# MLP weights in runs of four, the bias loaded as rows, and products that stream 64 columns, at the end of a decode kernel

## The chip, the cores and the metric

The kernel runs on one core of one Trainium2 chip. The metric is device time in microseconds (us). A run also states its span, the time from the first to the last profiled instruction; the time is usually 1.3 to 1.6 us longer than the span. Because that difference has nothing to do with the instructions studied here, I quote spans beside times where tenths matter. All runs compared are fast; two runs near 672 us are slow and left out.

Words used: TensorE multiplies (the profile's PE is its products, PEld its weight loads), VectorE is DVE, ScalarE is ACT, SP issues most DMAs. "Landing" is the moment when the last of a DMA's shares has counted up its semaphore; the records show 16 such counts for each weight load. The "granted clock" is the share of TensorE's full clock that the record shows, here always 1.00 or 0.50.

## The reference

One decode step of a transformer layer for 4 sequences with one token each: attention over a cache of 4096 positions and 32 heads, then an MLP with the Mish activation.

```
x = A_x                                     # (4, 1, 640)
q = layernorm(x) @ wq                       # 640 -> 32 heads x 128
p = softmax(q . k_cache * 128**-0.5)        # 4 x 32 heads x 4096 positions
h = x + (p . v_cache) @ wo                  # 4096 -> 640
a = layernorm(h) @ w1 + b1                  # 640 -> 1728
a = a * tanh(softplus(a))
out = h + a @ w2                            # 1728 -> 640
```

In bf16 the two caches are 268 MB, the weights 15 MB. Everything must be read once.

## The kernel before

One DMA queue (SP) streams wq, then the K and V caches tile by tile, then wo, w1 and w2, in that order and nearly without a gap. The parts that matter here are the loads outside this queue and the work after the last V tile. In the wo and w1 products only 4 columns (the batch) are streamed against each 128 x 128 weight block:

```
FM = F // P                                   # 13 whole blocks of 128 MLP units, and 64 left over
# b1: unit 13*p + j sits at partition p, column j: 128 rows of 26 bytes, and 64 of 2 bytes
load(ac, b1T[:, 0:FM], B_b1[0 : FM * P].rearrange("(p j) -> p j", j=FM), "b1a", "S")
load(ac, b1T[0:FT, FM : FM + 1], B_b1[FM * P : F].rearrange("(p o) -> p o", o=1), "b1b", "S")
...
W2S = (0, 6, 10, 12, FM)                      # w2 arrives in chunks of 6, 4, 2 and 1 rows a partition
...
# attention output: 32 rows of wo, 5 blocks each
w = wo_sb[:, k, j, :].rearrange("p (m c) -> p c m", c=DC)[:, c, :]          # weight columns 5 apart: 10 bytes
mm(y_ps[:, c, :], w, a_t[:, k, j, :], False, done, "y" if done else None)   # 4 columns
...
# first MLP product: 14 blocks of units, 5 parts of the contraction, loaded as parts 0-1, 2-3, 4
w = w1_sb[:, c, 0 : FM * P].rearrange("p (f j) -> p j f", j=FM)[:, j, :]    # weight columns 13 apart: 26 bytes
mm(h1_ps[0 : (P if j < FM else FT), j, :], w, cen[:, c, :], False, done, ...)  # 4 columns
...
# second MLP product: the activations are the weights (4 columns), w2 streams 160 columns to each of 4 column strips
```

The softmax here doesn't subtract the row's maximum and nothing guards it: scores larger than these inputs give would overflow.

## Time and profile before

The median before was 662.52 us (662.31 to 663.42), the span of the profiled run 661.0 us.

The slice table of the page: the span in 40 slices, the granted TensorE clock and the busy share of the DMA engines in tenths, then the GB/s moved.

```profile
PEclk9998698879659796869668778977965879786865
DMA  9999999999999999999999999999999999999997
GB/s 386 444 440 444 421 408 445 437 441 437 429 420 440 436 436 436 440 428 424 444 432 432 440 428 424 444 432 433 444 436 432 424 440 428 440 440 428 412 418 303
```

DMA is at 9 (90% or more) in every slice but the last. This kernel lasts as long as its bytes take. The queue table says which queue: columns are packets, megabytes and the share of all 16 engines' time.

```profile
q1 hardware_dynamic: 6784, 283.27, 99.2%
q10 hardware_dynamic: 328, 0.09, 0.1%
```

Queue 1 is SP. Queue 10 belongs to ScalarE and carries x, the last 64 rows of w2, and b1. The DMA view lists issues with KB and the us from issue to landing; three lines of it:

```profile
slotA<-in_B_w_dram SPq DMA_DIRECT2D x1, 160.0 KB, 15.9
...
b1T<-in_B_b_dram ACTq DMA_DIRECT2D x1, 3.2 KB, 29.1
b1T<-in_B_b_dram ACTq DMA_DIRECT2D x1, 0.1 KB, 38.4
```

The last row of w2 (160 KB) is issued at 641.91 and lands at about 657.8; b1 lands 29 and 38 us after its issue at 3.4 and 3.8.

The chain of waits, cut to its last links (start, duration, what):

```profile
628.31 23.43 DMA slotB<-in_B_w_dram
...
651.78 3.07 PE red L714 x44
...
656.69 2.16 PE red L714 x55
...
658.87 0.33 DVE o_bf L710
```

Read backwards: o_bf, the output's conversion, waited for 2.16 us of TensorE (w2), that for the activation, and that for 3.07 us of TensorE (w1) which began when the second chunk of w1 had landed at 651.7. In this chain TensorE is the last thing that o_bf waits for. The timeline of TensorE shows the products themselves (start, duration, form, count, and in brackets the idle time before them):

```profile
638.95 1.76 PE L714 MATMUL y_ps<-a_t,slotB 128*128 128x4 bf16 x40
...
644.59 3.56 PE L714 MATMUL y_ps<-a_t,slotB 128*128 128x4 bf16 x80
...
649.76 3.93 PE L714 MATMUL red<-cen,slotB 128*64 128x4 bf16 x56 [0.30 <-DMA slotB<-in_B_w_dram]
...
653.74 1.10 PE L714 MATMUL red<-cen,slotB 128*64 128x4 bf16 x14
...
656.69 0.30 PE L714 MATMUL red<-w_tail,act 64*4 64x160 bf16 x4 [1.10 <-DVE act L703]
656.92 1.90 PE L714 MATMUL red<-slotA,act 128*4 128x160 bf16 x52
```

The 70 w1 products start 59 to 63 ns apart, the 160 wo products 40 ns apart, and four w2 products (one row) every 133 ns. o_bf began at 658.87, 1.03 us after the last row of w2 had landed (657.84 by the semaphore records).

The windows view, cut at the clock's own steps of 3.41 us (columns: window, its length, then busy time and instruction count of PE, PEld, DVE, ACT, POOL; granted clock; DMA share; GB/s):

```profile
639.85:643.26 3.41, 3.41 (x72) 3.38 (x70) 1.41 (x3) 1.10 (x1) 0.00 (x0) 1.00 1.01 426
643.26:646.67 3.41, 3.19 (x68) 2.89 (x66) 0.37 (x2) 0.00 (x0) 0.00 (x0) 0.50 1.01 413
646.67:650.09 3.42, 2.77 (x41) 2.51 (x40) 1.27 (x9) 0.18 (x1) 0.00 (x0) 0.50 1.01 417
650.09:653.50 3.41, 3.29 (x54) 3.19 (x53) 0.68 (x5) 1.40 (x2) 0.00 (x0) 0.50 1.04 432
653.50:656.90 3.40, 2.30 (x64) 1.89 (x62) 1.53 (x6) 0.25 (x1) 0.00 (x0) 0.50 0.84 334
```

The granted clock is 1.00 in one step and then 0.50 to the end, though PE is busy for 2.30 to 3.41 us of each step; most of the products stream 4 columns.

### The profile page before, as it was taken

The page shows a single profiled execution, that of the slowest core. Times are in us where ns is not written, and L with a number is a line of the kernel's source. Part 1 is how long each engine was busy: PE and PEld are TensorE (multiplying, and loading weights), DVE is VectorE, ACT ScalarE, POOL GpSimd, SP SyncE. Part 2 cuts the span into 40 slices and gives each one's busy share as a digit, 9 for nine tenths or more (in the row PEclk, how much of TensorE's full clock was granted, in tenths as well). Part 3 has the DMA queues.
Part 4 walks back from the last instruction along what each step waited for, and adds up shares of the span by engine and source line. Part 5 has one row for each costly group of instructions (what it writes and reads, how often), then busy time and mean ns, then how long its engine had stood idle before and what let it go on. Part 6 is the DMA issues. An engine that isn't in the chain of part 4 may idle for free. (4 is left out here: it accounts for less than half of the span.)

```text
span 661.0 us, 4948 instructions
## 1 busy us (share of the span) xinstructions
PE 386.6 (58%) x2623; PEld 70.5 (11%) x1663; DVE 407.4 (62%) x255; ACT 40.7 (6%) x157; POOL 1.7 (0%) x12
## 2 busy tenths in 40 slices
PE   0356667457317595838307485828534757675877
PEld 0100010101101010101100010100110001010146
DVE  2067889386049778677219688948306798857612
ACT  0200000000000000000000000000000000000011
POOL 0000000000000000000000000000000000000000
PEclk9998698879659796869668778977965879786865
DMA  9999999999999999999999999999999999999997
GB/s 386 444 440 444 421 408 445 437 441 437 429 420 440 436 436 436 440 428 424 444 432 432 440 428 424 444 432 433 444 436 432 424 440 428 440 440 428 412 418 303
DMA packets 7121, 283.48 MB, mean 429 GB/s; under 512 B 1028, under 2 KB 1352, under 8 KB 2376
## 3 DMA queue, kind: packets, MB, share of 16 engines
q1 hardware_dynamic: 6784, 283.27, 99.2%
q10 hardware_dynamic: 328, 0.09, 0.1%
q8 instruction: 6, 0.10, 0.1%
q14 instruction: 3, 0.02, 0.0%
HBM read 283.35 MB, written 0.01 MB: 429 GB/s over the span
## 5 line engine op out<-in xcount | busy, mean ns | idle before, releaser
L513 DVE TENSOR_TENSOR slotA<-slotA,q_bc 128x8192 bf16<-128x8192 bf16 x32 | 140.6, 4415 | 106.2 <-DMA slotA<-in_A_k_cache_dram 106.2
L513 DVE TENSOR_TENSOR slotB<-slotB,q_bc 128x8192 bf16<-128x8192 bf16 x32 | 140.7, 4416 | 17.6 <-DMA slotB<-in_A_k_cache_dram 17.6
L524 DVE TENSOR_REDUCE s_f<-red 128x64 f32<-128x1024 f32 x64 | 78.0, 1218 | 96.8 <-PE red L724 96.8
L724 PE MATMUL red<-slotA,ident 128*128 128x512 bf16 x480 | 135.3, 445 | 0.0
L724 PE MATMUL red<-slotB,ident 128*128 128x512 bf16 x480 | 127.4, 425 | 0.0
L714 PE MATMUL red<-slotA,ident 128*128 128x512 bf16 x32 | 14.4, 451 | 127.7 <-PEq L49 127.7
L714 PE MATMUL pv<-slotC,e 128*32 128x512 bf16 x768 | 52.9, 436 | 37.4 <-PEq L49 34.4
L714 PE MATMUL red<-slotB,ident 128*128 128x512 bf16 x32 | 14.1, 441 | 88.3 <-PEq L49 88.3
L393 ACT ACTIVATE ex<-s_f 128x64 bf16<-128x64 f32 x64 | 16.4, 256 | 513.3 <-DVE s_f L524 513.3
L538 DVE TENSOR_TENSOR e<-ex,hmask 128x512 bf16<-128x512 bf16 x64 | 39.8, 683 | 0.0
L714 PEld LDWEIGHTS pv<-slotC,e 128*32 128x32 bf16 x768 | 22.6, 107 | 94.3 <-issue 80.7
L714 PEld LDWEIGHTS red<-slotA,ident 128*128 128x128 bf16 x32 | 3.2, 99 | 195.7 <-issue 195.7
L714 PEld LDWEIGHTS red<-slotB,ident 128*128 128x128 bf16 x32 | 3.2, 99 | 172.1 <-issue 172.1
L714 PEld LDWEIGHTS o_ps<-pv_sb,selo 128*32 128x32 f32 x136 | 13.5, 109 | 64.5 <-issue 64.5
L714 PE MATMUL o_ps<-pv_sb,selo 128*32 128x128 f32 x136 | 18.0, 276 | 0.0
L714 PE MATMUL pv<-slotA,e 128*32 128x512 bf16 x256 | 14.5, 380 | 0.3 <-PEq L49 0.3
L403 ACT COPY pv_sb<-pv 128x512 f32<-128x512 f32 x16 | 9.4, 585 | 68.6 <-PE pv L714 68.6
L393 ACT ACTIVATION_READ_ACCUMULATOR ex<-s_f 128x1 f32 x64 | 11.9, 186 | 0.0
L714 PEld LDWEIGHTS pv<-slotA,e 128*32 128x32 bf16 x256 | 6.7, 97 | 23.4 <-issue 17.5
L563 DVE RECIPROCAL rl<-misc 32x1 f32<-32x1 f32 x4 | 0.6, 150 | 12.7 <-PE misc L714 12.7
L714 PE MATMUL red<-slotC,lnT 128*32 128x512 bf16 x40 | 4.5, 629 | 6.7 <-PEq L49 6.7
L714 PE MATMUL y_ps<-a_t,slotB 128*128 128x4 bf16 x160 | 7.0, 179 | 0.2
(99 smaller groups left out, 67.2 us busy)
## 6 DMA issues: line engine op xcount, KB each, us to landing
slotC<-in_A_v_cache_dram SPq DMA_DIRECT2D x2, 4096.0 KB, 39.3
slotC<-in_A_wq_dram SPq DMA_DIRECT2D x1, 5120.0 KB, 16.4
slotB<-in_A_wo_dram SPq DMA_DIRECT2D x3, 1280.0 KB, 15.9
slotB<-in_B_w_dram SPq DMA_DIRECT2D x2, 864.0 KB, 22.6
slotA<-in_B_w_dram SPq DMA_DIRECT2D x1, 960.0 KB, 20.8
slotB<-in_A_wo_dram SPq DMA_DIRECT2D x1, 640.0 KB, 19.6
slotA<-in_B_w_dram SPq DMA_DIRECT2D x1, 640.0 KB, 19.7
slotB<-in_A_wo_dram SPq DMA_DIRECT2D x1, 480.0 KB, 20.3
```

What stands on the lines that cost most here:

```text
L393: lambda: a.activation(out=ex[:, sl], in_=s_f[:, sl], func=ACT.Exp, scale=SCALE, accum_out=rs[:, b, s : s + 1],),
L403: lambda: a.copy(out=pv_sb[:, :, :].rearrange("p r d -> p (r d)"), in_=pv[:, :]),
L513: lambda: v.tensor_tensor(out=t, in0=t, in1=q_bc[:, hg, b, :].unsqueeze(1).to_broadcast([P, RS, Dh]), op=ALU.mult,),
L524: lambda: v.tensor_reduce(out=s_f[:, s * RS : (s + 1) * RS], in_=red[:, k : k + 2, :].rearrange("p k (r c) -> p (k r) c", c=CW), axis=AX.X ...
L538: lambda: v.tensor_tensor(out=e[:, sl, :], in0=ex[:, sl].unsqueeze(2).to_broadcast([P, RS, G]), in1=hmask[:, :].unsqueeze(1).to_broadcast( ...
L563: dv.do(lambda: v.reciprocal(out=rl[:, :], in_=l_ps), ("rl", hg), DV)
L714: lambda: nc.tensor.matmul(out_, lhsT=lhsT, rhs=rhs, start=start, stop=stop, skip_group_check=skip),
L724: return t.add_instruction(mybir.InstMatmult(name=nc.get_next_instruction_name(), engine=mybir.EngineType.PE, ins=[t.lower_ap(rhs), t.lowe ...
```

## The change

The intent: w1 products that start less than 60 ns apart, by weight columns 8 bytes apart instead of 26; a TensorE clock that stays at 1.00 beyond 643.26, by wider products; and no 192 tiny DMA packets, by b1 as rows. The w2 rows follow the new order of units, in chunks of 4, 4, 4 and 1 rows.

```diff
+    FI = 4                    # units in runs of 4
+    FB = FM // FI
+    F0 = FB * FI * P
+    WD = 16                   # batch columns repeated 16 times
+    y_w = y_full[:, 0 : DC * WD * N].rearrange("p (c w n) -> p c w n", w=WD, n=N)
+    y_ps = y_w[:, :, 0, :]
+    h1_w = red[:, 2:4, :].rearrange("p k (j w n) -> p (k j) w n", w=WD, n=N)
+    h1_ps = h1_w[:, 0:FC, 0, :]
-    W2S = (0, 6, 10, 12, FM)
+    W2S = tuple(range(0, FM, FI)) + (FM,)
...
-            sp.need(("PV", i - 1) if hg else ("qb", N - 1))
+            sp.need(("PV", i - 1) if hg else "b1p")
...
-        load(ac, b1T[:, 0:FM], B_b1[0 : FM * P].rearrange("(p j) -> p j", j=FM), "b1a", "S")
-        load(ac, b1T[0:FT, FM : FM + 1], B_b1[FM * P : F].rearrange("(p o) -> p o", o=1), "b1b", "S")
+        load(ac, b1r[:, :], B_b1[0:F0].rearrange("(k f) -> k f", k=FB), "b1a", "B0")
+        load(ac, b1e[:, :], B_b1[F0:F].rearrange("(o f) -> o f", o=1), "b1b", "B1")
...                            # six small transposes on TensorE and two copies make b1T
-                    mm(y_ps[:, c, :], w, a_t[:, k, j, :], False, done, "y" if done else None)
+                    mm(
+                        y_w[:, c, :, :], w, a_t[:, k, j, :].unsqueeze(1).to_broadcast([P, WD, N]),
+                        False, done, "y" if done else None,
+                    )
-        mm(red[:, 2, 0 : FC * N], ident[:, :], zeros[:, 0 : FC * N], True, False)
+        for k in (2, 3):
+            mm(red[:, k, :], ident[:, :], zeros[:, 0:1].to_broadcast([P, 512]), True, False)
...
-                        w = w1_sb[:, c, 0 : FM * P].rearrange("p (f j) -> p j f", j=FM)[:, j, :]
+                        k, i = divmod(j, FI)
+                        w = w1_sb[:, c, k * FI * P : (k + 1) * FI * P]
+                        w = w.rearrange("p (f i) -> p i f", i=FI)[:, i, :]
...
-                        h1_ps[0 : (P if j < FM else FT), j, :], w, cen[:, c, :], False, done,
+                        h1_w[0 : (P if j < FM else FT), j, :, :], w,
+                        cen[:, c, :].unsqueeze(1).to_broadcast([P, WD, N]), False, done,
...                            # cut: loads of w2, start of y, bias products, semaphores
```

More of the change, by code (lines that the diff above doesn't have):

```diff
@@ L122 @@
     WSEM = ["WQ", "WT"] + [f"W{k}" for k in range(13)]
-    for s in ["PE", "DV", "DVP", "DVA", "AC", "ACP", "PO", "KA", "KB", "VA", "VC", "V2", "X", "S", "OUT0", "OUT1", "FIN"] + WSEM:
+    for s in ["PE", "DV", "DVP", "DVA", "AC", "ACP", "PO", "KA", "KB", "VA", "VC", "V2", "X", "B0", "B1", "OUT0", "OUT1", "FIN"] + WSEM:
         book.handles[s] = nc.alloc_semaphore(s)
@@ L173 @@
     wq = slot["C"][:, 0 : DC * H * Dh].rearrange("p (c n) -> p c n", c=DC)
+    b1r = sb("b1r", (FB, FI * P), BF16, setup, topC)
+    b1e = sb("b1e", (1, F - F0), BF16, setup, topC)
     x_bf = sb("x_bf", (N, D), BF16, setup, topC)
@@ L222 @@
     y_full = nc.alloc_psum_tensor("y_ps", (P, 512), FP32).ap()
-    y_ps = y_full[:, 0 : DC * N].rearrange("p (c n) -> p c n", n=N)
+    WD = 16
+    y_w = y_full[:, 0 : DC * WD * N].rearrange("p (c w n) -> p c w n", w=WD, n=N)
+    y_ps = y_w[:, :, 0, :]
     tpl = misc[:, 0 : DC * N].rearrange("p (c n) -> p c n", n=N)
@@ L226 @@
     l_ps = misc[0:BG, 64:65]
+    b1_ps = pv[:, 0:FC]
     a_ps = misc[:, 128 : 128 + G * N].rearrange("p (j n) -> p j n", n=N)
@@ L229 @@
     sq_ps = pv[:, 0 : DC * N]
-    h1_ps = red[:, 2, 0 : FC * N].rearrange("p (j n) -> p j n", n=N)
+    h1_w = red[:, 2:4, :].rearrange("p k (j w n) -> p (k j) w n", w=WD, n=N)
+    h1_ps = h1_w[:, 0:FC, 0, :]
     y2_ps = red[:, 0, 0:OC]
@@ L246 @@
     dv = Prog(nc.vector, book)
-    pe = Prog(nc.tensor, book, take=["DVP", "DVA", "ACP", "VA", "VC", "V2"] + WSEM)
+    pe = Prog(nc.tensor, book, take=["DVP", "DVA", "ACP", "VA", "VC", "V2"] + WSEM + ["B0", "B1"])
     def tiles(src, i):
@@ L330, in sync_prog @@
         sp.need(("PV", NT - 2))
-        w2_v = B_w2[0 : FM * P, :].rearrange("(p j) n -> p j n", j=FM)
         for k, (j0, j1) in enumerate(zip(W2S, W2S[1:])):
-            load(sp, w2_sb[:, j0:j1, :], w2_v[:, j0:j1, :], ("w2", j0), f"W{len(WOS) + len(W1S) - 1 + k}")
+            load(
+                sp, w2_sb[:, j0:j1, :],
+                B_w2[j0 * P : j1 * P, :].rearrange("(p j) n -> p j n", j=j1 - j0), ("w2", j0),
+                f"W{len(WOS) + len(W1S) - 1 + k}",
+            )
         store(sp, 0)
@@ L357, in act_prog @@
         a = nc.scalar
-        ac.need("b1z")
-        load(ac, b1T[:, 0:FM], B_b1[0 : FM * P].rearrange("(p j) -> p j", j=FM), "b1a", "S")
-        load(ac, b1T[0:FT, FM : FM + 1], B_b1[FM * P : F].rearrange("(p o) -> p o", o=1), "b1b", "S")
+        load(ac, b1r[:, :], B_b1[0:F0].rearrange("(k f) -> k f", k=FB), "b1a", "B0")
+        load(ac, b1e[:, :], B_b1[F0:F].rearrange("(o f) -> o f", o=1), "b1b", "B1")
         ac.need("eps", "mv")
@@ L504, in dve_prog @@
         dv.do(lambda: v.tensor_copy(out=xT[:, :, :], in_=tpx[:, :, :]), "xT", DVP)
+        dv.need("b1p", "b1z")
+        dv.do(lambda: v.tensor_copy(out=b1T[:, 0:FM], in_=b1_ps[:, 0:FM]), "b1m", DV)
+        dv.do(lambda: v.tensor_copy(out=b1T[0:FT, FM:FC], in_=b1_ps[0:FT, FM:FC]), "b1T", DVP)
         dv.do(lambda: v.memset(rsm[:, :, :], 1.0), ("rsm", -1), DVP)
@@ L649, in dve_prog @@
         dv.do(lambda: v.tensor_copy(out=h_hi[:, :, :], in_=st[:, :, :]), "h_hi", DV)
-        dv.need("std2", "b1b")
+        dv.need("std2")
         dv.do(
@@ L749, in pe_setup @@
         pe.need("xT")
-        mm(y_full[:, 0 : DC * N], ident[:, :], xT[:, :, :].rearrange("p c n -> p (c n)"), True, False)
+        mm(y_w, ident[:, :], xT[:, :, :].unsqueeze(2).to_broadcast([P, DC, WD, N]), True, False)
         pe.need("lnT", "wq")
@@ L768, in pe_setup @@
             )
+        pe.need("b1a", "b1b")
+        for k in range(FI):
+            mm(
+                b1_ps[:, k : FB * FI : FI], b1r[:, :].rearrange("k (f i) -> k i f", i=FI)[:, k, :],
+                ident[0:FB, 0:FB], True, True,
+            )
+        mm(b1_ps[:, FM - 1 : FM], b1e[:, 0:P], ident[0:1, 0:1], True, True)
+        mm(b1_ps[0:FT, FM:FC], b1e[:, P : P + FT], ident[0:1, 0:1], True, True, "b1p")
     def fold(i, s):
@@ L856, in wo_mm @@
                     done = k == NHG - 1 and j == G - 1 and c == DC - 1
-                    mm(y_ps[:, c, :], w, a_t[:, k, j, :], False, done, "y" if done else None)
+                    mm(
+                        y_w[:, c, :, :], w, a_t[:, k, j, :].unsqueeze(1).to_broadcast([P, WD, N]),
+                        False, done, "y" if done else None,
+                    )
         hg = NHG - 1
@@ L879, in pe_tail @@
                 for part in (b1_hi, b1_lo):
-                    mm(
-                        red[:, 2, 0 : FC * N], ident[:, :], part[:, :, :].rearrange("p j n -> p (j n)"),
-                        False, False,
-                    )
+                    for j0, j1 in ((0, FC // 2 + 1), (FC // 2 + 1, FC)):
+                        mm(h1_ps[:, j0:j1, :], ident[:, :], part[:, j0:j1, :], False, False)
             pe.need(("w1", c0))
@@ L886, in pe_tail @@
                 for c in range(c0, c1):
-                    if j < FM:
-                        w = w1_sb[:, c, 0 : FM * P].rearrange("p (f j) -> p j f", j=FM)[:, j, :]
+                    if j < FB * FI:
+                        k, i = divmod(j, FI)
+                        w = w1_sb[:, c, k * FI * P : (k + 1) * FI * P]
+                        w = w.rearrange("p (f i) -> p i f", i=FI)[:, i, :]
                     else:
-                        w = w1_sb[:, c, FM * P : F]
+                        w = w1_sb[:, c, j * P : min((j + 1) * P, F)]
                     done = c == DC - 1 and j == FM - 1
                     mm(
-                        h1_ps[0 : (P if j < FM else FT), j, :], w, cen[:, c, :], False, done,
+                        h1_w[0 : (P if j < FM else FT), j, :, :], w,
+                        cen[:, c, :].unsqueeze(1).to_broadcast([P, WD, N]), False, done,
                         "h1_ps" if done else None,
@@ L926, in pe_prog @@
         pe_setup()
-        pe.need("selo", "xT")
+        pe.need("selo", "xT", "b1T")
         logs = []
```

## The prediction

> **What bounds the kernel now.** The DMA stream. The slice table shows DMA at 9 tenths or more in all slices but the last, mean 429 GB/s, 283.48 MB, 99.2% on one queue. By the trace's landing records the last weight chunk (one row of w2) lands at 657.84 us of a 661.0 us span. The change moves none of these bytes and touches none of the waits that pace the K/V loads.
>
> **The tail.** The chain of waits ends: DMA of w1 until 651.7, TensorE 3.07, VectorE/ScalarE activation 1.8, TensorE w2 2.16 (to 658.85), o_bf 0.33, store. With w2's last row landing at 657.84, even a free TensorE could start o_bf only near 658.2, not 658.87. That 0.65 us, 0.1% of the span, is the most that the tail can give.
>
> **The change.**
> - w1 weights at a column step of 8 bytes instead of 26. In the timeline w1 products start every 59 to 63 ns; wo products (step 10 bytes) every 40 ns at either clock; the om transposes (step 16 bytes) every 62. [...]
> - 64 streamed columns instead of 4. The windows view grants 1.00 from 639.85 to 643.26, then 0.50 to the end. [...] the trace shows only these two, in steps of 3.41 us. Counting streamed columns in this trace, a step at full clock keeps it above about 0.35. The repeated wo (estimate 0.4 to 0.55) should keep it; layernorm gap and w1 (estimate 0.28) are a toss-up. At half clock a product takes about 53 ns (512 columns take 427), so wo 2 and 3 would lose up to 1 us; at full clock nothing. If it holds to w2, a w2 row goes from 133 ns to about 70.
> - Zeroing two full banks: about +0.5 us TensorE. Two more bias products: 0.1 us.
> - b1 as 4 rows: the 192 packets took 1.73 us summed over 16 engines, 0.1 us of stream; they landed at 42 us, needed at 650. Small transposes and the V(0) load now wait for b1; I expect it by 22 us, before qb at 23.6, while K(1) is in flight to 55: free.
> - w2 chunks of 4,4,4,1 rows for 6,4,2,1: same bytes; rows 8 to 11 arrive near 657.45.
>
> **On the critical path.** w1's second chunk lands at 651.73, its third at 652.80, so w1 can end near 653.6 to 654.1 instead of 654.76. w2 then starts near 655.7 and waits for landings. Of some 3 us of TensorE work saved, 0.3 to 0.65 us reach the end; if the clock falls during wo, about nothing.
>
> **Prediction.** 662.0 us (before 662.52), 8 in 10 between 661.3 and 662.9. Faster by over 2%: 0.01; within 2%: 0.98; slower: 0.01.
>
> **What would show it.** w1 products every 33 to 40 ns at full clock (53 at half); clock 1.0 from 643 to 647; last w2 landing still 657.5 to 658.1; a chain that ends with the DMA of w2 just before the last products, o_bf near 658.2 to 658.5; DMA share unchanged.
>
> **What would make it wrong.** b1 landing after 35 us, holding the first products; the last landing moving by a microsecond (16 KB instruction fetches take 0.95 us each; two fell after 646); the clock at half, so that wo runs late.

The forecast came to 662.0 us: of some 3 us of TensorE work saved, 0.3 to 0.65 us were to reach the end. By the paces that the runs below measured, 33 ns instead of 60, the 70 w1 products are worth up to 1.9 us; the 13 w2 rows, at 69 ns instead of 133, make another 0.8. The 33 in "What would show it" was my estimate.

## The result and the profile after

The median after was 661.38 us (661.26 to 662.32, 4 runs) against 662.41 us before. The ratio is 0.9984 with a 95% interval of 0.9967 to 1.0001; a ratio here is the mean time of one kernel's fast runs over that of the other's of the same rounds, so not quite the ratio of the medians quoted. The verdict is "same" at the 2% level. The medians lie 1.0 us apart, which is twice the predicted 0.5 us. The interval includes no difference at all. The spans show one more clearly: nine runs of the kernel after (here and in its repetition below) have 659.8 to 660.8, median 660.0, and 34 of the kernel before 660.6 to 661.3, median 661.0.

The queue table after:

```profile
q1 hardware_dynamic: 6784, 283.27, 99.4%
...
q10 hardware_dynamic: 112, 0.09, 0.0%
```

Queue 10 went from 328 packets to 112; SP's queue is unchanged. The chain of waits now ends with the stream:

```profile
639.18 17.80 DMA slotA<-in_B_w_dram
...
657.02 0.68 PE red L728 x20
...
657.73 0.32 DVE o_bf L724
```

The third chunk of w2 lands at 656.98, then TensorE needs only 0.68 us, and o_bf follows at 657.73. TensorE in the tail:

```profile
638.32 1.78 PE L728 MATMUL y_ps<-a_t,slotB 128*128 128x64 bf16 x40
...
644.12 3.61 PE L728 MATMUL y_ps<-a_t,slotB 128*128 128x64 bf16 x80
...
649.35 1.19 PE L728 MATMUL red<-cen,slotB 128*64 128x64 bf16 x28 [0.65 <-DMA slotB<-in_B_w_dram]
651.32 1.64 PE L728 MATMUL red<-cen,slotB 128*64 128x64 bf16 x28 [0.78 <-DMA slotB<-in_B_w_dram]
...
652.99 1.08 PE L728 MATMUL red<-cen,slotB 128*64 128x64 bf16 x14
...
655.92 0.24 PE L728 MATMUL red<-w_tail,act 64*4 64x160 bf16 x4 [1.09 <-DVE act L717]
656.09 0.72 PE L728 MATMUL red<-slotA,act 128*4 128x160 bf16 x32
657.02 0.65 PE L728 MATMUL red<-slotA,act 128*4 128x160 bf16 x20 [0.21 <-DMA slotA<-in_B_w_dram]
```

The wo products kept their 40 ns and are no slower for 16 times the columns. The first w1 chunk starts a product every 33 ns, most of the second and all of the third every 53 ns. A w2 row takes 69 ns instead of 133, and TensorE now idles 0.21 us for the landing of the third chunk. The windows at this run's clock steps:

```profile
641.50:644.90 3.40, 3.20 (x64) 2.83 (x63) 1.49 (x3) 0.00 (x0) 0.00 (x0) 1.00 0.98 409
644.90:648.30 3.40, 3.06 (x67) 2.84 (x65) 0.44 (x3) 0.00 (x0) 0.00 (x0) 1.00 1.04 425
648.30:651.70 3.40, 1.97 (x39) 1.69 (x39) 1.43 (x11) 1.58 (x2) 0.00 (x0) 1.00 1.00 416
651.70:655.10 3.40, 3.13 (x84) 2.76 (x81) 0.82 (x4) 0.25 (x1) 0.00 (x0) 0.51 1.02 416
655.10:658.50 3.40, 1.54 (x56) 0.93 (x56) 1.04 (x3) 0.00 (x0) 0.00 (x0) 0.99 0.32 127
```

The clock was 1.00 until 651.75, fell to 0.50 for one step, and was back at 1.00 for w2. The two w1 paces go with it: the products start 33 ns apart up to 651.75 and 53 ns apart after it. For 64 columns at half clock, 53 ns is also what I estimate from the cache phase, where 512 columns take 427 ns at that clock (216 at full). The 33 ns is also the pace of e3 below, with 4 columns at half clock.

From the semaphore records I took the landings and o_bf of both profiles. "Mean" is the mean over the 16 shares of the last DMA, which scatters less than the slowest share.

```
                          before    after
last w2 row, mean share   656.85    656.55     -0.30
last w2 row, landing      657.84    657.39     -0.45
o_bf starts               658.87    657.73     -1.14
landing to o_bf             1.03      0.34     -0.69
span                      661.02    659.86     -1.16
```

Two things came together: the stream ended earlier, and TensorE followed it more closely. How much of the first belongs to the change is settled under e2.

### The profile page after: what moved, and what is told of

The parts are those of the page before. It is cut to its first block, busy times and chain, and to the rows that moved or that the text cites. A ratio compares the mean times of both kernels' runs of the same rounds, so it can differ in the third digit from the quotient of the medians.

```text
span 659.9 us, 4968 instructions
## 1 busy us (share of the span) xinstructions
PE 382.4 (58%) x2630; PEld 68.6 (10%) x1672; DVE 407.7 (62%) x257; ACT 40.7 (6%) x157; POOL 1.7 (0%) x12
## 5 line engine op out<-in xcount | busy, mean ns | idle before, releaser
L738 PE MATMUL red<-slotA,ident 128*128 128x512 bf16 x480 | 137.3, 450 | 0.0
L738 PE MATMUL red<-slotB,ident 128*128 128x512 bf16 x480 | 124.5, 418 | 0.0
L728 PE MATMUL red<-slotA,ident 128*128 128x512 bf16 x32 | 14.5, 452 | 128.5 <-PEq L49 128.5
L728 PE MATMUL red<-slotB,ident 128*128 128x512 bf16 x32 | 14.0, 437 | 86.9 <-PEq L49 86.9
L517 DVE CAST b1T<-pv 128x13 bf16<-128x13 f32 x1 | 0.2, 174 | 13.1 <-PE pv L728 13.1
```

The source lines that it names most:

```text
L517: dv.do(lambda: v.tensor_copy(out=b1T[:, 0:FM], in_=b1_ps[:, 0:FM]), "b1m", DV)
L728: lambda: nc.tensor.matmul(out_, lhsT=lhsT, rhs=rhs, start=start, stop=stop, skip_group_check=skip),
L738: return t.add_instruction(mybir.InstMatmult(name=nc.get_next_instruction_name(), engine=mybir.EngineType.PE, ins=[t.lower_ap(rhs), t.lowe ...
```

## The experiments

My theory: the end is the last landing plus what TensorE still has to do. The b1 packets move the landing; runs of 4, the columns and the clock move the rest. The rivals are that the earlier landing is scatter between executions, that one part alone does everything, and that TensorE still limits the tail after the change. All times are medians of fast runs. Each group of runs was timed against the kernel before on the same chip, at 662.46, 662.53 and 662.52 us; 34 fast runs of it in these groups have spans of 660.6 to 661.3, median 661.0.

### e1: only b1 as a row

```diff
 # on the kernel before
-        load(ac, b1T[:, 0:FM], ...)          # 128 rows of 26 bytes
-        load(ac, b1T[0:FT, FM : FM + 1], ...) # 64 rows of 2 bytes
+        load(ac, b1r[:, :], B_b1.rearrange("(o f) -> o f", o=1), "b1a", "B0")
+        # 14 small transposes on TensorE after qb, two copies into b1T
```

> The kernel before with b1 loaded as one row and transposed on TensorE; weights and columns as before. The step from before to after was 1.0 us, of which the profiles put 0.69 us after the last w2 landing and 0.45 us into an earlier last landing (657.84 to 657.39). Theory A (the 192 tiny b1 packets cost the stream 0.45 us): the last w2 landing comes near 657.4 and the time falls by 0.45 us to about 662.0. Theory B (they cost only their own 1.73 us over 16 engines, 0.1 us, and the rest is scatter of the first loads): the landing follows the landing of wq, K(0) minus wq is about 0.1 us shorter, time lower by 0.1 us only. Distance from landing to o_bf stays 1.0 us in both.

Measured: 662.07 us (the reported median of 662.17 includes the slow run), spans 660.6 to 661.1, median 660.7. In the profile the mean share of the last landing is 656.58 and o_bf starts 1.02 us after the landing. So the stream ends earlier and the work after it has not moved. In time it is 0.3 to 0.4 us, between the 0.45 us of theory A and the 0.1 us of theory B. The test that was named for theory B came out for it: from the mean share of wq's landing to that of K(0)'s it is 19.29 us here and 19.39 in the kernel before, 0.10 us shorter. The landing of wq itself came 0.21 us earlier than in the profile before (15.19 against 15.40).

### e2: four copies of the tiny loads added

```diff
 # on the kernel after
+        for k in range(4):
+            load(ac, b1d[:, k, 0:FM], B_b1[0 : FM * P].rearrange("(p j) -> p j", j=FM), ("b1x", k), "S")
+            load(ac, b1d[0:FT, k, FM : FM + 1], B_b1[FM * P : F].rearrange("(p o) -> p o", o=1), ("b1y", k), "S")
...
-        dv.need("std2")
+        dv.need("std2", ("b1y", 3))
```

> The kernel after with four copies of the old b1 loads (768 tiny packets) added into a tile nobody reads, waited for late. Theory A: 0.45 us for each 192 packets, so the last landing and the time move by +1.8 us (about 663.2). Theory B: 0.1 us each, +0.4 us (about 661.8). If packets are free: 661.4.

Measured: 662.45 us, span median 660.9, which is 1.07 us and 0.9 us over the kernel after: between the theories again. The mean shares of the landings say more, if the last one is measured from that of wq:

```
copies  run             wq      last w2 row   between
0       after           15.18   656.55        641.37
0       after again     15.19   656.55        641.36
0       e1              15.19   656.58        641.39
0       e3              15.32   656.68        641.36
0       e5              15.07   656.34        641.27
0       e7              15.15   656.50        641.35
1       before          15.40   656.85        641.45
1       before again    15.27   656.71        641.44
1       e4              15.19   656.88        641.69
4       e2              15.17   657.45        642.28
```

Without copies the mean between the two is 641.35 us. One copy adds 0.10 and 0.09 us in the two profiles of the kernel before and 0.34 in e4; four add 0.93, or 0.23 each. The packets themselves are booked at 9 ns each, 1.73 us for 192, or 0.11 us when spread over 16 engines. So theory B's 0.1 us is what the kernel before paid; e2 and e4 paid more, 0.23 and 0.34 for each copy. The rest of the difference in last landings was there when wq landed. Most of it is older than the packets: the 80 KB of w2 that precede them in their queue landed (mean share) at 12.83 and 12.70 us in the kernel before and at 12.48 to 12.76 in the other eight, and the first tiny packet moved at 13.13. Of the landing's 0.45 us in the first pair of profiles, 0.21 is this earlier wq, 0.08 lies between wq and the last row, and 0.15 is scatter of the slowest share. Only the 0.08 can be put down to the packets.

The packet records of the kernel before show why b1 took so long to land: its 128 packets of 26 bytes stretch from 13.1 to 29.6 us, and from 14.6 us on they come back every 2.42 us, which is the length of one 64 KB packet of the SP queue. Whether each such change of queue costs time beyond the packet, and why e4 paid more than the kernel before for the same packets, stays open; no run here measures it by itself.

### e3: the kernel after with 4 columns

```diff
 # on the kernel after
-    WD = 16
+    WD = 1
-    h1_w = red[:, 2:4, :].rearrange("p k (j w n) -> p (k j) w n", w=WD, n=N)
+    h1_w = red[:, 2, 0 : FC * N].rearrange("p (j w n) -> p j w n", w=WD, n=N)
-        for k in (2, 3):
-            mm(red[:, k, :], ident[:, :], zeros[:, 0:1].to_broadcast([P, 512]), True, False)
+        mm(red[:, 2, 0 : FC * N], ident[:, :], zeros[:, 0 : FC * N], True, False)
...            # the bias products in one piece again
```

> The kernel after with 4 streamed columns again, runs of 4 and b1 rows kept. Theory that both parts are needed: granted clock 0.5 from about 643 on; wo 40 ns, w1 about 33 ns, a w2 row 133 ns; w1 ends earlier than in after (653.2 against 654.0, as 53 ns products vanish), but the last four w2 rows at 133 ns and the slower end put o_bf about 0.6 us after the last landing instead of 0.34: time +0.2 to +0.3 us on after. Rival (the columns gave most of the 0.69 us): landing to o_bf back near 1.0 us, +0.6 us.

Measured: 661.63 us, spans 660.1 to 660.4, median 660.1. TensorE:

```profile
649.62 1.16 PE L728 MATMUL red<-cen,slotB 128*64 128x4 bf16 x28 [0.29 <-DMA slotB<-in_B_w_dram]
...
652.83 0.73 PE L728 MATMUL red<-cen,slotB 128*64 128x4 bf16 x14
...
655.65 1.24 PE L728 MATMUL red<-slotA,act 128*4 128x160 bf16 x32
657.30 0.84 PE L728 MATMUL red<-slotA,act 128*4 128x160 bf16 x20 [0.41 <-DMA slotA<-in_B_w_dram]
```

The clock was 0.50 from 641.6 on. The w1 products still start 33 ns apart within a chunk: the same pace at half clock as the first chunk had at full clock in the kernel after. The w2 rows take 133 ns, and o_bf starts 0.53 us after the landing, so my theory of this run holds. The span is only 0.1 us over the median of the kernel after. The step from e1 (span 660.7, step of 26 bytes, 4 columns, one row of b1) to e3 (660.1) is the runs of 4 with their chunks of w2: 0.6 us, the largest single part of the change. No run separates the step from the chunks. The traces speak for the step: w2's first product (the 64-row tail) starts at 655.42 here and at 656.31 in e1, because w1 ends earlier.

### e4: only the 64 columns

```diff
 # on the kernel before
+    WD = 16                                   # y_w, h1_w, wide zeroing as in the change
-                    mm(y_ps[:, c, :], w, a_t[:, k, j, :], ...)
+                    mm(y_w[:, c, :, :], w, a_t[:, k, j, :].unsqueeze(1).to_broadcast([P, WD, N]), ...)
-                        h1_ps[0 : (P if j < FM else FT), j, :], w, cen[:, c, :], ...
+                        h1_w[0 : (P if j < FM else FT), j, :, :], w, cen[:, c, :].unsqueeze(1).to_broadcast([P, WD, N]), ...
```

> The kernel before with 64 streamed columns alone; w1 step 26 bytes and tiny b1 loads stay. If the last landing is a floor that either part almost reaches: w1 near 60 ns, clock 1.0 at w2 or not by chance, o_bf 0.35 to 0.65 us after the last landing, time 0.4 to 0.6 us below before. If the runs of 4 are what matters: landing to o_bf stays near 1.0 us and the time is that of before.

Measured: 662.54 us, span median 661.0: the kernel before. The expected 0.4 to 0.6 us did not come; the runs of 4 are what matters.

```profile
649.96 4.02 PE L717 MATMUL red<-cen,slotB 128*64 128x64 bf16 x56 [0.44 <-DMA slotB<-in_B_w_dram]
...
657.29 1.90 PE L717 MATMUL red<-slotA,act 128*4 128x160 bf16 x52
```

The w1 products stay at 60 ns, so w1 ends later than its last chunk lands, and w2 cannot start before 657.05. In this profile the clock fell to 0.50 at 651.1, so w2 took as long as before (1.90 us), and o_bf started 1.21 us after the landing.

### e5: a quarter of the wo and w1 products

```diff
 # on the kernel after; wrong result on purpose (relative error 0.026)
                 for c in range(DC):
+                    if j % 4 != 3:
+                        continue              # wo
...
                 for c in range(c0, c1):
+                    if j % 4 != 0:
+                        continue              # w1
```

> The kernel after with three quarters of the wo and w1 products left out (wrong result on purpose; loads, waits and the last weight row are kept). If the end of the DMA stream is the floor and the kernel after already sits on it: w1 and h end a microsecond earlier, landing to o_bf stays 0.3 to 0.35 us, time 661.4 within 0.2. If TensorE still bounds the tail: 0.3 us or more below after.

Measured: 661.78 us, spans 660.2 to 660.7, median 660.4. With three quarters of these products gone the kernel is 0.4 us slower, not faster. h started at 653.01, a microsecond earlier than in the kernel after. But the clock fell to 0.50 at 645.5, after a step in which the products streamed 0.16 of the columns that the clock allows; w2 rows took 133 ns again, and o_bf started 0.53 us after the landing, as in e3. So the amount of wo and w1 work no longer bounds the tail; what is left after the landing depends on the clock. The expected 0.3 to 0.35 us had left out the clock.

### The two kernels again

> The kernel after unchanged, for a second profile: 661.4; last landing 657.2 to 657.6, mean landing of its 16 shares near 656.55. If the clock at w2 is luck of the phase it may be 0.5 here, with landing to o_bf near 0.55 us and 0.2 us more time; else 0.34 again.

> The kernel before unchanged, for a second profile: 662.4; if the 0.27 us for the tiny packets is right, the mean landing of the last chunk is near 656.87 again and landing to o_bf near 1.0; if the first loads scatter by 0.3 us between executions, it moves by that much.

The kernel before repeated itself: 662.37 us, span median 660.9, o_bf 1.04 us after the landing. The mean share of the last landing was 656.71, not the 656.87 that would have confirmed 0.27 us for the packets (the 0.27 us that e6 starts from too); it moved with the landing of wq, 0.13 us earlier than in the first profile. The kernel after: 661.39 us, but its profiled run had a span of 660.7, not 659.9, with the same mean share of the last landing (656.55). Its clock steps in the tail:

```profile
646.80:650.20 3.40, 2.61 (x53) 2.39 (x51) 1.56 (x12) 0.71 (x2) 0.00 (x0) 1.00 1.01 416
650.20:653.60 3.40, 2.78 (x50) 2.46 (x46) 0.32 (x4) 0.87 (x1) 0.00 (x0) 0.50 1.04 430
653.60:657.00 3.40, 2.30 (x74) 1.88 (x77) 1.54 (x6) 0.25 (x1) 0.00 (x0) 0.50 0.74 296
```

And its TensorE:

```profile
651.55 1.82 PE L728 MATMUL red<-cen,slotB 128*64 128x64 bf16 x28 [0.62 <-DMA slotB<-in_B_w_dram]
...
656.56 1.90 PE L728 MATMUL red<-slotA,act 128*4 128x160 bf16 x52
```

Here the clock closed at 650.2 and stayed at 0.50. All of the second w1 chunk ran at 53 ns and all 13 w2 rows at 133 ns. o_bf started 0.91 us after the landing, not 0.34; I had expected 0.55 for this case. In e3, with 4 columns, the clock was at 0.50 as well, and it was 0.53: where the clock closes, the 64 columns hurt, because w1 then takes 53 ns a product instead of 33. The nine runs of the kernel after have spans 659.8, 659.8, 659.9, 660.0, 660.0, 660.0, 660.1, 660.7 and 660.8: two groups.

### e6: the tail of w2 on the SP queue behind w1

```diff
 # on the kernel after
-        load(ac, w2_tail[0:FT, :], B_w2[FM * P : F, :], "w2t", "WT")     # beside wq, at the start
+        load(sp, w2_tail[0:FT, :], B_w2[FM * P : F, :], "w2t", "WT")     # after the w1 loads
```

> The kernel after with the 80 KB tail of w2 loaded on the same queue as all other weights, behind w1, not beside wq on the other queue. Same bytes. If small packets on a second queue cost the stream more than their own time, as 192 tiny ones did (0.27 us measured against 0.1 us booked): wq packets of 1640 ns return towards 1514 ns, the last landing comes 0.3 to 0.4 us earlier, time near 661.0. If what costs is bytes alone: 661.4.

Measured: 661.81 us, span median 660.4, so slower than the kernel after. The mean share of wq landed at 14.45 instead of 15.18 us, as expected, but that of the last landing at 656.79 instead of 656.55. The lead was still 0.30 us at the last w1 chunk and was gone after these 80 KB. So the expected gain of 0.3 to 0.4 us failed. Why they cost more there than their bytes is open. The clock was 0.50 from 649.2 on, which goes with the 0.54 us from landing to o_bf.

### e7: filler products in the waits of the tail

```diff
 # on the kernel after
+        def fill(n):
+            for _ in range(n):
+                mm(o_full, ident[:, :], zeros[:, 0:1].to_broadcast([P, 512]), True, True)
...
         mm(sq_ps, ones_d[:, :], sq[:, :, :].rearrange("p c n -> p (c n)"), True, True, "sqm")
+        fill(2)
...            # after the products of the first w1 chunk
+            if c0 == 0:
+                fill(2)
...
+        fill(4)
         pe.need("act")
```

> The kernel after with eight filler products of 512 columns (zeros, into a PSUM bank nobody reads) in the waits of the tail: two in the layernorm gap, two after the first w1 chunk, four while the activation runs. In the two profiles of after the clock fell to 0.5 at 650 to 652 and w2 ran at 1.0 in one (landing to o_bf 0.34, span 659.9) and at 0.5 in the other (0.91, 660.7). If the clock at w2 is what splits the runs of after: with fillers the granted clock stays 1.0 to the end, landing to o_bf 0.3 to 0.35, all spans 659.7 to 660.1, none near 660.7. Rival (the split comes from something else, as instruction fetches): spans still split, 660.7 in about one of four.

Measured: 661.41 us (661.17 to 661.48), spans 659.8 to 660.0 in all five runs. The clock steps and the end of TensorE's timeline:

```profile
646.60:650.00 3.40, 2.99 (x52) 2.37 (x50) 1.43 (x11) 0.58 (x2) 0.00 (x0) 1.00 1.02 421
650.00:653.40 3.40, 3.00 (x70) 2.38 (x66) 0.45 (x4) 1.00 (x1) 0.00 (x0) 1.00 1.04 427
653.40:656.80 3.40, 2.52 (x84) 1.39 (x80) 1.54 (x6) 0.25 (x1) 0.00 (x0) 1.00 0.80 317
```

```profile
653.99 1.04 PE L728 MATMUL o_ps<-zeros,ident 128*128 128x512 bf16 x4
...
655.54 0.72 PE L728 MATMUL red<-slotA,act 128*4 128x160 bf16 x32
657.22 0.65 PE L728 MATMUL red<-slotA,act 128*4 128x160 bf16 x20 [0.96 <-DMA slotA<-in_B_w_dram]
```

The clock stayed 1.00 to the end. The fillers (653.99) fit into the wait for the activation. The w1 products start 33 ns apart, w2 waits 0.96 us for the third chunk, and o_bf starts 0.34 us after the landing. The last landing was as late here (657.58) as in the second profile of the kernel after (657.61), yet the span is 660.0, not 660.7: the difference is the clock at w2. With the clock held, none of five runs has the longer span, nor any of the five of e9 below. Two runs of nine against none of ten is little evidence on its own; the traces, in which the clock and the distance from landing to o_bf go together, carry the argument.

### e8 and e9: the tail of w2 behind wq, without and with fillers

```diff
 # on the kernel after (e9: on e7)
-        load(ac, w2_tail[0:FT, :], B_w2[FM * P : F, :], "w2t", "WT")
+        load(sp, w2_tail[0:FT, :], B_w2[FM * P : F, :], "w2t", "WT")     # directly behind wq
```

> The kernel after with the 80 KB w2 tail on the same queue as the rest, right behind wq (behind w1 it gained 0.73 us at wq, then lost more than that at the end). If sharing the engines between two queues is what costs: mean landing of the last chunk 0.3 to 0.5 us earlier than 656.55, span near 659.6 in fast-clock runs. If the bytes cost the same wherever they are: 656.5, span 660.0.

> Both together: a candidate to beat both kernels. If both theories hold: clock 1.0 to the end, spans near 659.5, time near 661.0 in every run. If only the fillers work: 659.9 and 661.35 without the runs near 662.3.

Measured for e8: 662.22 us, spans 660.1 to 660.8, median 660.4, so 0.4 us over the kernel after; its profile fell on a slow run and is not used, so the reason is not shown. Measured for e9: 661.36 us (661.18 to 661.40), spans 659.8 to 660.0, clock 1.00 to the end, mean share of the last landing 656.47 against 656.50 in e7. In these two profiles the bytes cost the same on either queue when they come at the start; the theory that sharing the engines between two queues costs 0.3 us or more for this load found no support. So e9 has what e7 has and nothing more. Both e7 and e9 are faster than the kernel before by 0.2% (ratios 0.9981 and 0.9980, intervals that end at 0.9994 and 0.9993). Against the kernel after their medians are level, and what they gain is that the longer runs are absent: mean span 659.9 against 660.1.

## Why the prediction was right, and where not

The predicted 662.0 us (661.3 to 662.9, within 2%) held; 661.38 us lies at the lower edge, 0.08 us inside. The range also held the kernel before itself, so that the number held says little; the terms say more.

- **The DMA stream bounds the kernel.** Right. Leaving out three quarters of the wo and w1 products (e5) gained nothing. The chain after the change ends with a w2 landing.
- **The tail can give at most 0.65 us.** The size was about right for this term: landing to o_bf fell by 0.69 us in the first pair of profiles. That is luck in part: with the clock closed it fell by only 0.13 us (1.04 to 0.91 in the second pair). By spans, the runs of 4 (0.6 us, e1 to e3) and the columns (0.1) came to the upper end of the 0.3 to 0.65 us of which the prediction took the middle. As a bound on the whole gain it failed, because it took the landing as fixed.
- **b1 as rows frees 0.1 us of stream.** Right in the traces of the kernel before: 0.10 and 0.09 us from wq on. In e4 the same packets cost 0.34 us, and four copies 0.93. The time of e1, though, fell by 0.3 to 0.4 us; the other 0.2 to 0.3 us is not explained by what the packets cost behind wq and stays open (wq's own landing scatters from 15.07 to 15.40 over the ten profiles of the table). So the 1.0 us between the medians is, by runs, 0.3 from the rows, 0.6 from the runs of 4 and 0.1 from the columns, and the first pair of traces accounts for about 0.8 of it (0.10 and 0.69). The predicted last landing of 657.5 to 658.1 and o_bf of 658.2 to 658.5 missed 657.39 and 657.73 mostly by the earlier wq and the scatter of the slowest share; the second profile of the kernel after landed inside (657.61).
- **w1 at 33 ns for a step of 8 bytes.** Right: 33 ns at half clock with 4 columns (e3) and at full clock with 64 (e7); 64 columns at half clock take 53. The paces of products with 128 x 128 bf16 weights are 33 ns at 8 bytes, 40 at 10 and 60 at 26, and all three were seen at either clock (8 bytes: e3 and e7; 10 bytes: the kernel before; 26 bytes: e4). Why the step matters was not shown; the 33 ns was my estimate.
- **64 columns hold the clock through wo; a toss-up after that.** Right in both profiles of the kernel after: once open (638.09 and 639.95) it was 1.00 through wo, then once back at 1.00 for w2 and once not. wo kept 40 ns, but for the first 21 products of the second profile, which ran at 53 before the clock opened. What the prediction lacked is what the toss is worth: 0.57 us from landing to o_bf between the two profiles (0.34 and 0.91), more than half of the whole gain. (Their spans differ by 0.8 us; the other 0.22 us is a later slowest share in the second.) On average the columns bring almost nothing: mean span 660.1 against 660.2 in e3.
- **b1 lands before it is needed.** Right: the b1 transposes ran at 22.24 us without holding anything, and the first K product still waited for its cache tile.
- **Wide zeroing costs about 0.5 us, and the extra bias products 0.1 us.** The two zeroing products took 0.45 us, partly inside the wait for the last heads; what was left was taken up by the wait for the last chunk of wo, so nothing of it reached the end.

What stays open: what opens and closes the clock. In the kernel before it closed at 643.26, after a step in which the profile shows PE busy for all of its 3.41 us with 72 products, most of 4 columns; by my count the columns streamed were 0.15 of what the clock allows. I counted streamed columns in each step, as a share of what the granted clock could stream (512 in 427 ns at half clock, twice as many at full). Over twelve traces, at full clock, steps above 0.38 kept the clock; between 0.27 and 0.38 some kept it and some lost it. At half clock, steps with 0.62 and 0.65 opened it in two runs, and steps with up to 0.88 did not in others. In the trace of the kernel before, from which I took my threshold of 0.35, one step with 0.31 kept the clock and one with 0.38 lost it. So the threshold is no rule. In columns, 0.88 at half clock is 0.44 at full clock: that did not always open a clock that every step above 0.38 kept open.

## What to carry to other kernels

In a kernel bound by its DMA stream, look first at the last landing and then at what is left to do after it: work removed before that point is worth nothing once the engines wait for it anyway (e5: 0.4 us slower), and a small load elsewhere can move the landing, here by 0.1 to 0.3 us for 192 packets booked at 0.11. The start of the stream scatters by as much before the packets move (12.48 to 12.83 us for the same 80 KB), so measure from a landing there. Weight columns 8 bytes apart instead of 26 made products start every 33 ns instead of 60 (at half clock only with few streamed columns). If the last products are held up by the clock, put harmless wide products into the waits before them (in e7 and e9 the clock stayed at 1.00 to the end); widening the real products left it to chance (landing to o_bf 0.34 us in one profile, 0.91 in the other).
